# A GpSimd mask put ahead of the next pair's B, and an x load moved from GpSimd's DMA queue to SyncE's, in a fused state-space and bilinear feed-forward kernel

## The chip, the cores and the metric

The kernel runs on one core of a Trainium2 chip. Its time is device microseconds of one execution; the figure compared is the median of several executions. A profiled execution, taken apart from these, gives the trace. Times below are microseconds from the start of the profiled span unless they say otherwise.

## The reference

Inputs are `x` (4, 8, 768, 32), `a` (4, 8, 768), `B` and `C` (4, 8, 768, 16), all float32, and three weight matrices of a feed-forward part. First a state-space scan is computed for each of 4 x 8 heads, then a bilinear feed-forward layer on all heads of a token.

```python
for c in range(nc):                      # chunks of 32 tokens
    cum = np.cumsum(la, axis=-1)         # la = log(clip(a))
    L = np.exp(cum[:, :, :, None] - cum[:, :, None, :]) * causal
    CB = np.einsum('bhin,bhjn->bhij', Cc, Bc)
    y_intra = np.einsum('bhij,bhjd->bhid', CB * L, xc)
    y_inter = np.einsum('bhin,bhnd->bhid', Cc, state) * np.exp(cum)[..., None]
    y[:, :, sl] = y_intra + y_inter
    Bx = np.einsum('bhjn,bhjd->bhjnd', Bc, xc) * decay_from_j[..., None, None]
    state = decay_full[:, :, None, None] * state + np.sum(Bx, axis=2)
...
a = x @ w_a                              # x: 3072 tokens x 256, from y
b = x @ w_b                              # 256 x 1536
return (a * b @ w_out).astype(np.float32)
```

## The kernel before

The 768 tokens are cut into six blocks of 128. A block of the four batches is handled as two pairs of batches, so there are twelve pairs, p = 0 to 11; pair p belongs to block p // 2. Pairs 0 to 3 use an older layout and finish before the stretch of interest; pairs 4 and up are the ones that matter here.

For such a pair p the steps are these.

- **Loads.** `loads_bc(p)` issues the loads of C and B (128 KB each) on SyncE's queue, and `loads_x(p)` the load of x (256 KB). `loads_x` takes the issuing engine as an argument: without one it is GpSimd, with `nc.sync` it is SyncE. Both end in line 156. The natural tiles (`bn`, `cn`, `xn`) have three buffers each.
- **Scaling on GpSimd.** `scale_bc(p, 1, nc.gpsimd)` multiplies C by its decay factors into half of a `planes` tile (line 295). `scale_bc(p, 0, nc.gpsimd)` does the same for B (line 303, tile `bm`) and spreads it into the other part of `planes` with two copies (line 313). There are two `planes` tiles, for even and odd pairs.
- **Turning.** `turn(p)` is one transposing DMA on SyncE's queue (line 347) from `planes` to the tile `turned`, which holds B and C with the state dimension on partitions.
- **`prep(p)`** is scale C, scale B, turn, in that order.
- **Scores.** `scores(p)` multiplies the turned C and B on TensorE into the four banks `SC` (line 357).
- **Masks.** Each of the four banks is multiplied by the causal mask into the tile `t`. Most are done by VectorE from the bank (line 412). With `by_pool=True` ScalarE copies the bank to `tmp` (line 409) and GpSimd multiplies (line 410).
- **x.** `scale_x(p, eng)` makes x in 16 bits, on ScalarE (line 286) or GpSimd (line 288, through `prep_x`).
- **Group.** `group(blk)` computes the outputs of a block's two pairs: state times C (line 507), masked scores times x (line 418), and the sums for the next state (line 446), and lets ScalarE evacuate them to `XB` (line 537).

The feed-forward part runs between these steps on TensorE: `unit` (line 600) and `bunit` (line 666) multiply by the first two weights, VectorE forms the product, and `out_half` (line 636) and `bout` (line 693) multiply by the third. Their results go through `osb` on ScalarE (lines 648 and 705) and are stored by SyncE's queue (lines 650 and 706).

The order of everything is written out by hand: the schedule is manual, each engine and each queue runs its instructions in the order in which the program emits them, and an instruction starts when those that it depends on are done. A step's place in the program therefore also sets its place in SyncE's queue, which carries the loads, the turnings and the stores in one order. Around pair 6 that order is: loads for pairs 6 and 7, three stores of block 0 and 1, turn(6), the store of `out_store(2, 1)`, x of pair 6, turn(7), x of pair 7, C and B of pair 8, two stores, C and B of pair 9, turn(8), turn(9), x of pair 9, C and B of pair 10.

Of the kernel before, what the change touches and what calls it, by code (L numbers as in the profile page):

```python
# [28 lines left out]
def kernel(  # L29
# [13 lines left out]
    nc = tc.nc  # L43
# [92 lines left out]
    def by_token(t_):  # L136
        return t_.rearrange("p h r n -> p (h r n)").rearrange("p (t h n) -> p t h n", t=2, h=H)
# [14 lines left out]
    def load2(eng, p, which):  # L152
        if p < P0:
            return [load1(eng, p, which, bt) for bt in range(2)]
        blk, bp = divmod(p, NBP)
        return eng.dma_start(  # L156
            by_token(pair_in[p][which]).rearrange("p t h n -> p (t h) n"),
            (B, C, x)[which][2 * bp : 2 * bp + 2, :, blk * Q : (blk + 1) * Q, :].rearrange("t h q n -> q (t h) n"),
        )
# [121 lines left out]
    def scale_x(p, eng):  # L281
        X16 = mid.tile([128, H, 2, D], f16, name="x16", tag="x16")
        xo, xi = X16.rearrange("p h r d -> p (h r d)"), pair_in[p][2].rearrange("p h r d -> p (h r d)")
        st.setdefault(p, {})["X16"] = X16
        if eng is nc.scalar:
            nc.scalar.mul(xo, xi, XS)
        else:
            eng.tensor_scalar(xo, xi, XS, None, ALU.mult)  # L288

    def scale_bc(p, which, eng, factor=None):  # L290
        blk, bp = divmod(p, NBP)
        name, f = (("bm", fB), ("cm", fC))[which]
        raw = by_token(pair_in[p][which]) if p >= P0 else pair_in[p][which].rearrange("p h r n -> p r h n")
        if p >= P0 and which:
            eng.tensor_tensor(  # L295
                out=planes[p % 2][:, 4:6].rearrange("p t (h n) -> p t h n", n=N),
                in0=raw,
                in1=f[:, blk, :, bp].unsqueeze(3).broadcast_to((128, 2, H, N)),
                op=ALU.mult,
            )  # L300
            return
        m_ = mid.tile([128, 2, H, N], f16, name=name, tag=name)
        eng.tensor_tensor(  # L303
            out=m_,
            in0=raw,
            in1=(f[:, blk, :, bp] if factor is None else factor).unsqueeze(3).broadcast_to((128, 2, H, N)),
            op=ALU.mult,
        )
        st.setdefault(p, {})[name] = m_
        if p >= P0:  # L310
            dst = planes[p % 2][:, 0:4].rearrange("p (t e) (m f n) -> p t e m f n", e=2, f=2, n=N)
            for e in range(2):
                eng.tensor_copy(dst[:, :, e, :, e], m_.rearrange("p t (m f) n -> p t m f n", f=2)[:, :, :, e])
# [31 lines left out]
    def turn(p):  # L345
        T_ = mid.tile([128, 6, 128], f16, name="turned", tag="turned")
        nc.sync.dma_start(T_, planes[p % 2].rearrange("p a c -> p (a c)"), transpose=True)  # L347
        st[p]["BT"] = T_[:, 0:4].rearrange("p (t e) k -> p e t k", e=2)
        st[p]["CT"] = T_[:, 4:6]

    def scores(p):
        BT, CT = st[p]["BT"], st[p]["CT"]
        st[p]["T1"] = mid.tile([128, H, 2, Q], f16, name="t1", tag="t1")
        for e, bt, m in itertools.product(range(2), range(2), range(4)) if p >= P0 else ():
            rows = slice(32 * m, 32 * m + 32)
            c0 = (e * 2 + bt) * Q
            nc.tensor.matmul(  # L357
                SC[m][:, c0 : c0 + Q],
                BT[rows, e, bt],
                CT[rows, bt],  # L360
                start=True,
                stop=True,
                skip_group_check=True,
                tile_position=(32 * m, 0),
            )
        for e in range(2) if p < P0 else ():
            for r in range(2):
                for m in range(4):
                    for bt in range(2):
                        rows = slice(32 * m, 32 * m + 32)  # L370
                        c0 = (e * 2 + r) * Q
                        nc.tensor.matmul(  # L372
                            SC[m][64 * bt : 64 * bt + 64, c0 : c0 + Q],
                            BT[rows, e, r, bt],
                            CT[rows, bt],
                            start=True,
                            stop=True,
                            skip_group_check=True,
                            tile_position=(32 * m, 64 * bt),
                        )  # L380

    def product(p, m):

        if p >= P0:
            return (
                st[p]["T1"][:, 2 * m : 2 * m + 2].rearrange("p e t q -> p (e t) q"),
                SC[m].rearrange("p (c q) -> p c q", q=Q),
            )
        return (
            st[p]["T1"][:, 2 * m : 2 * m + 2].rearrange("p e r q -> p e (r q)"),  # L390
            SC[m].rearrange("p (e c) -> p e c", e=2),
        )
# [8 lines left out]
    def mask(out_in, by_pool=False, by_token=False):  # L401
        o_, i_ = out_in
        if by_token:
            c_ = causal_q.unsqueeze(1).broadcast_to((128, 4, Q))
        else:
            c_ = causal.rearrange("p r q -> p (r q)").unsqueeze(1).broadcast_to((128, 2, 2 * Q))
        if by_pool:
            tmp = mid.tile([128, *c_.shape[1:]], f32, name="tmp", tag="tmp")
            nc.scalar.copy(tmp, i_)  # L409
            nc.gpsimd.tensor_tensor(out=o_, in0=tmp, in1=c_, op=ALU.mult)  # L410
        else:
            nc.vector.tensor_tensor(out=o_, in0=i_, in1=c_, op=ALU.mult)  # L412
# [155 lines left out]
    def state_spread(p):  # L568
        blk, bp = divmod(p, NBP)
        if p + NBP < P0:  # L570
            Sbd = mid.tile([128, 2, H * D], f16, name="sbd", tag="sbd")
            nc.gpsimd.tensor_tensor(
                out=Sbd.rearrange("p t (m c) -> p t m c", m=4),
                in0=U32[:, p].unsqueeze(2).broadcast_to((128, 2, 4, 2 * D)),
                in1=maskbd.rearrange("p (m e) d -> p m (e d)", e=2).unsqueeze(1).broadcast_to((128, 2, 4, 2 * D)),
                op=ALU.mult,
            )
        else:
            Sbd = mid.tile([128, 2, 2 * D], f16, name="spair", tag="spair")
            nc.gpsimd.tensor_tensor(  # L580
                out=Sbd.rearrange("p t (e d) -> p t e d", e=2),
                in0=U32[:, p].rearrange("p t (e d) -> p t e d", e=2),
                in1=par.unsqueeze(1).unsqueeze(3).broadcast_to((128, 2, 2, D)),
                op=ALU.mult,
            )
        if blk + 1 < NG:
            nc.gpsimd.tensor_tensor(
                out=gU[:, p + NBP],
                in0=U32[:, p],
                in1=G[:, 2 * bp : 2 * bp + 2, blk + 1].unsqueeze(2).broadcast_to((128, 2, 2 * D)),  # L590
                op=ALU.mult,
            )
        st.setdefault(("S", p + NBP), {})["Sbd"] = Sbd
# [120 lines left out]
    def loads_x(p, eng=None):  # L714
        if p < NP:
            load2(eng or nc.gpsimd, p, 2)
# [148 lines left out]
    def prep(p, spread=()):  # L865
        if p < NP:
            scale_bc(p, 1, nc.gpsimd)
            scale_bc(p, 0, nc.gpsimd)
            turn(p)
        for q in spread:  # L870
            if q // NBP < NBLK - 1:
                state_spread(q)

    def prep_x(p):
        if p < NP:
            scale_x(p, nc.gpsimd)
# [9 lines left out]
    def stage(p, by_pool, spread=()):  # L886
        scores(p)
        if p % NBP == 0 and p // NBP + 1 < NBLK:
            fb(p // NBP + 1)
        if by_pool:  # L890
            mask(product(p, 3), by_pool=True, by_token=True)
        for q in spread:
            if q // NBP < NBLK - 1:
                state_spread(q)

    def masked(p, ms, *units):
        for i in range(max(len(ms), len(units))):
            h = units[i]() if i < len(units) else None
            if i < len(ms):
                mask(product(p, ms[i]), by_token=True)  # L900
            if h:
                h()
# [36 lines left out]
    scores(4)  # L939
    mask(product(4, 3), by_pool=True, by_token=True)  # L940
    scale_x(5, nc.scalar)
    prep(6)
    masked(4, (0, 1))
    out_mm(2, 1, o_ps, range(6, NK))
    out_store(2, 1, o_ps)()
# [1 line left out]
    go((3, 1))  # L947
    scores(5)
    mask(product(5, 3), by_pool=True, by_token=True)
    mask(product(5, 2), by_pool=True, by_token=True)  # L950
    loads_x(6, nc.sync)
    prep(7)
# [5 lines left out]
    out_half(3, 1)  # L958

    stage(6, True, (4, 5))  # L960
    loads_x(8)
    prep_x(7)
    masked(6, (0, 1))
    masked(6, (2,), *bu(2, 0, 1, 2))
# [2 lines left out]
    stage(7, True)  # L967
    loads_bc(9)
    prep(8)
    prep(9)  # L970
    loads_x(9, nc.sync)
    loads_bc(10)
# [74 lines left out]
```

## Time and profile before

| | |
|---|---|
| Median of 3 runs | 125.01 us (124.95 to 126.14) |
| Profiled execution, its own time | 125.89 us |
| Span of the profile | 124.2 us |
| TensorE busy | 117.6 us, 95% |
| VectorE busy | 85.4 us, 69% |
| ScalarE busy | 71.6 us, 58% |
| GpSimd busy | 64.2 us, 52% |
| HBM read and written | 11.13 MB and 3.15 MB |
| Loads of C and B by SyncE (128 KB), issue to landing | 4.0 and 4.3 us, medians of 8 |
| Turnings, issue to landing | 3.9 us, median of 8 |

Times of the page are from one profiled execution, which was 0.88 us longer than the median of the runs; a difference read from the trace is carried over to the median as a difference. In the profile PE is TensorE, DVE VectorE, ACT ScalarE, POOL GpSimd and SP SyncE; a `q` behind an engine's name means its sequencer or DMA queue. A row of the timeline has the start, the time, engine, line, operation, tiles and count, and in brackets the idle time of that engine just before and what ended it. For a DMA the row is the time that its issue took, not the transfer.

### The profile page before, as it was taken

The numbers are of one execution on the slowest core, as the hardware profiler recorded it, in microseconds if no ns is written. First come the engines' busy times: TensorE is split into PE (matmuls) and PEld (weight loads), VectorE is DVE, ScalarE is ACT, GpSimd is POOL, SyncE is SP. The second block draws the span as 40 slices with busy tenths as digits, with TensorE's granted clock in tenths as the row PEclk, the third lists the DMA queues.
The fourth block names the chain that finished last, engine by engine and source line by source line (L and its number), as shares of the span: only waits on it lengthen the run. The fifth ranks groups of instructions, "written<-read, shape, count | busy, mean of one in ns | idle before, by whom it ended". The sixth has DMA issues, their size and how long they took to land.

```text
span 124.2 us, 3750 instructions
## 1 busy us (share of the span) xinstructions
PE 117.6 (95%) x1471; PEld 79.9 (64%) x1471; DVE 85.4 (69%) x162; ACT 71.6 (58%) x142; POOL 64.2 (52%) x109
## 2 busy tenths in 40 slices
PE   5887999999999998999999999999999999999990
PEld 2444788988888886844457456657464775555890
DVE  1886787885978589399983989848789544747200
ACT  0464845784645684788658755683637746657220
POOL 7999699947992479467735768114920000000000
PEclk9999999999999999999999999999999999999999
DMA  3999999997989699999886797369831012010122
GB/s 66 169 154 232 171 190 132 206 154 78 98 109 224 98 97 184 110 162 134 103 136 97 54 133 135 64 68 132 176 122 48 0 42 84 5 42 0 42 84 84
DMA packets 64753, 13.73 MB, mean 111 GB/s; under 512 B 59568, under 2 KB 64336, under 8 KB 64736
## 3 DMA queue, kind: packets, MB, share of 16 engines
q1 hardware_dynamic: 60528, 9.27, 48.8%
q0 software_dynamic: 2208, 3.87, 17.8%
q10 hardware_dynamic: 2000, 0.36, 1.6%
q8 instruction: 11, 0.18, 0.6%
q14 instruction: 6, 0.05, 0.1%
HBM read 11.13 MB, written 3.15 MB: 115 GB/s over the span
## 4 chain that ended last, share of the span: by engine, by line
PE 63%; DMA 17%; POOL 7%; SPq 7%; issue 3%; DVE 1%; ACT 1%; POOLq 0%; ACTq 0%; DVEq 0%
PE ops L693 15%; PE aps L666 13%; PE bps L666 13%; DMA bn<-in_B_dram 8%; PE aps L600 6%; PE bps L600 5%; DMA Wa<-in_moe_w_a_dram 5%; PE ops L636 4%; SPq L347 4%; DMA turned<-planes 3%; SPq L156 3%; POOL bm L303 1%; PE SC L357 1%; POOL cn L147 1%; PE SC L432 1%
## 5 line engine op out<-in xcount | busy, mean ns | idle before, releaser
L614 ACT COPY asb<-aps 128x512 f32<-128x512 f32 x72 | 41.9, 586 | 15.0 <-PE aps L666 9.7
L678 DVE TENSOR_TENSOR hkb<-bps,asb 128x512 f16<-128x512 f32 x48 | 32.3, 687 | 12.9 <-ACT asb L614 11.8
L666 PE MATMUL aps<-XB,Wa 128*128 128x512 f16 x96 | 28.6, 379 | 0.0
L666 PE MATMUL bps<-XB,Wb 128*128 128x512 f16 x96 | 28.5, 379 | 0.0
L693 PE MATMUL ops<-Wo,hkb 128*128 128x256 f16 (+1 forms) x204 | 22.5, 267 | 0.0
L693 PEld LDWEIGHTS <-hkb 128*128 128x128 f16 x204 | 18.5, 98 | 3.1
L412 DVE TENSOR_TENSOR t<-SC,causal_q 128x512 f16<-128x512 f32 x26 | 16.6, 681 | 5.1 <-PE SC L357 5.1
L621 DVE TENSOR_TENSOR hk<-bps,asb 128x512 f16<-128x512 f32 x24 | 16.1, 683 | 3.5 <-ACT asb L614 3.1
L666 PEld LDWEIGHTS <-Wb 128*128 128x128 f16 x96 | 9.9, 103 | 11.0 <-issue 0.3
L666 PEld LDWEIGHTS <-Wa 128*128 128x128 f16 x96 | 9.7, 103 | 9.1 <-issue 0.2
L600 PE MATMUL aps<-X2T,Wa 128*128 128x256 f16 x96 | 14.3, 274 | 1.0 <-DMA Wa<-in_moe_w_a_dram 0.7
L705 ACT ACTIVATE osb<-ops 128x256 f32<-128x256 f32 (+1 forms) x16 | 6.0, 376 | 14.4 <-PE ops L693 14.2
L600 PE MATMUL bps<-X2T,Wb 128*128 128x256 f16 x96 | 14.1, 273 | 0.0
L288 POOL TENSOR_SCALAR x<-xn 128x512 f16<-128x512 f32 x7 | 10.4, 1489 | 6.1 <-DMA xn<-in_x_dram 5.9
L636 PE MATMUL ops<-Wo,hk 128*128 128x256 f16 x96 | 11.6, 273 | 0.0
L600 PEld LDWEIGHTS <-Wa 128*128 128x128 f16 x96 | 9.3, 104 | 2.5 <-DMA Wa<-in_moe_w_a_dram 1.2
L600 PEld LDWEIGHTS <-Wb 128*128 128x128 f16 x96 | 9.8, 103 | 0.7
L636 PEld LDWEIGHTS <-hk 128*128 128x128 f16 x96 | 8.9, 98 | 1.5 <-DVE hk L621 0.2
L412 DVE TENSOR_TENSOR t<-SC,causal 128x512 f16<-128x512 f32 x13 | 8.2, 682 | 1.8 <-PE SC L372 1.7
L303 POOL TENSOR_TENSOR bm<-bn,fB 128x256 f16<-128x256 f32 x11 | 7.0, 640 | 4.6 <-DMA bn<-in_B_dram 2.8
L410 POOL TENSOR_TENSOR t<-tmp,causal_q 128x512 f16<-128x512 f32 x6 | 6.9, 1159 | 3.7 <-ACT tmp L409 3.6
L295 POOL TENSOR_TENSOR planes<-cn,fC 128x256 f16<-128x256 f32 x8 | 5.0, 623 | 7.2 <-DMA cn<-in_C_dram 7.0
(94 smaller groups left out, 118.2 us busy)
## 6 DMA issues: line engine op xcount, KB each, us to landing
out_dram<-osb SPq DMA_DIRECT2D x23, 128.0 KB, 1.9
xn<-in_x_dram SPq DMA_DIRECT2D x6, 256.0 KB, 4.9
cn<-in_C_dram SPq DMA_DIRECT2D x8, 128.0 KB, 4.0
bn<-in_B_dram SPq DMA_DIRECT2D x8, 128.0 KB, 4.3
Wa<-in_moe_w_a_dram POOLq DMA_DIRECT2D x2, 384.0 KB, 6.9
Wb<-in_moe_w_b_dram POOLq DMA_DIRECT2D x2, 384.0 KB, 8.2
Wo<-in_moe_w_out_dram POOLq DMA_DIRECT2D x2, 384.0 KB, 6.8
xn<-in_x_dram POOLq DMA_DIRECT2D x4, 128.0 KB, 7.3
```

What stands on the lines that cost most here:

```text
L288: eng.tensor_scalar(xo, xi, XS, None, ALU.mult)
L303: eng.tensor_tensor(out=m_, in0=raw, in1=(f[:, blk, :, bp] if factor is None else factor).unsqueeze(3).broadcast_to((128, 2, H, N)), op=AL ...
L410: nc.gpsimd.tensor_tensor(out=o_, in0=tmp, in1=c_, op=ALU.mult)
L412: nc.vector.tensor_tensor(out=o_, in0=i_, in1=c_, op=ALU.mult)
L600: nc.tensor.matmul(ps[:, kk * 2 * Q : (kk + 1) * 2 * Q], W[k // 6][:, f, k % 6 // 3 * 384 : (k % 6 // 3 + 1) * 384].rearrange("p (c kk) -> ...
L614: (nc.vector.tensor_copy if on_dve else nc.scalar.copy)(asb, a_ps)
L621: nc.vector.tensor_tensor(out=s["hk"][:, 2 * k2 : 2 * k2 + 2, :].rearrange("p k q -> p (k q)"), in0=b_ps, in1=asb, op=ALU.mult)
L636: nc.tensor.matmul(o_ps[:, 0:d_model], hk[:, k, bt * Q : (bt + 1) * Q], Wo[:, k, :], start=(k == 0), stop=(k == NK - 1), skip_group_check= ...
L666: nc.tensor.matmul(t_, W[k // 6][:, f, k % 6 // 3 * 384 : (k % 6 // 3 + 1) * 384].rearrange("p (c kk) -> p kk c", kk=3)[:, k % 3], XB[:, b ...
L678: return lambda: nc.vector.tensor_tensor(out=s["hk"][:, k], in0=ps[1], in1=asb, op=ALU.mult)
L693: nc.tensor.matmul(o_ps[:, 0:w], hk[:, k, c * Q : (c + 1) * Q], Wo[:, k, cs], start=(k == 0), stop=(k == NK - 1), skip_group_check=True,)
L705: nc.scalar.activation(out=o_sb[:, 0:w], in_=o_ps[:, 0:w], func=AF.Copy, scale=1.0 / (YS * YS))
```

## The change

Two steps are moved; no arithmetic is added or removed.

First, `prep(6)`, which stood after the GpSimd mask of pair 4, is taken apart. The scaling of C of pair 6 stays there. The scaling of B of pair 6 and the turning of pair 6 now stand after the first of the two GpSimd masks of pair 5 and ahead of the second. On GpSimd the first mask of pair 5 changes places with B of pair 6. On SyncE's queue turn(6), emitted later than before, now comes behind the store of `out_store(2, 1)`.

Second, the load of x of pair 8 is no longer issued by GpSimd at the start of pair 6's stage, but by SyncE between the turnings of pairs 8 and 9.

```diff
     scores(4)
     mask(product(4, 3), by_pool=True, by_token=True)
     scale_x(5, nc.scalar)
-    prep(6)
+    scale_bc(6, 1, nc.gpsimd)
     masked(4, (0, 1))
     out_mm(2, 1, o_ps, range(6, NK))
     out_store(2, 1, o_ps)()
     masked(4, (2,), *pu(3, 0))
     go((3, 1))
     scores(5)
     mask(product(5, 3), by_pool=True, by_token=True)
+    scale_bc(6, 0, nc.gpsimd)
+    turn(6)
     mask(product(5, 2), by_pool=True, by_token=True)
     loads_x(6, nc.sync)
     prep(7)
...
     stage(6, True, (4, 5))
-    loads_x(8)
     prep_x(7)
...
     stage(7, True)
     loads_bc(9)
     prep(8)
+    loads_x(8, nc.sync)
     prep(9)
     loads_x(9, nc.sync)
     loads_bc(10)
```

## Prediction

> **What bounds the kernel now.** I read the page's busy row first, then the chain that ended last, then the waits of TensorE, then the timelines of GpSimd and of SyncE's queue around those waits.
>
> ```profile
> PE 117.6 (95%) x1471; PEld 79.9 (64%) x1471; DVE 85.4 (69%) x162; ACT 71.6 (58%) x142; POOL 64.2 (52%) x109
> ```
>
> ```profile
> PE SC L418 <- POOL t L410: 0.5, 1, 0.5
> PE SC L357 <- DMA turned<-planes: 0.2, 1, 0.2
> ```
>
> TensorE is busy for 95% of the span. The second fence is the waits of TensorE from 32 us to the end (waited for: us in total, times, longest): these two are all, and the change touches nothing before 44 us. So only two stalls can be removed: one on a mask made by GpSimd, one on a turned tile. TensorE's timeline places them:
>
> ```profile
> 48.53 0.52 PE L418 MATMUL SC<-t,x 128*32 128x128 f16 x24
> 49.52 0.29 PE L418 MATMUL SC<-t,x 128*32 128x128 f16 x8 [0.47 <-POOL t L410]
> 49.63 0.30 PE L446 MATMUL SC<-x,bm 128*32 128x64 f16 x16
> 49.87 2.79 PE L636 MATMUL ops<-Wo,hk 128*128 128x256 f16 x24
> 52.59 0.40 PE L357 MATMUL SC<-turned 32*128 32x128 f16 x16
> ...
> 68.00 0.40 PE L357 MATMUL SC<-turned 32*128 32x128 f16 x16 [0.16 <-DMA turned<-planes]
> ```
>
> The first is at 49.52, in the outputs of block 2: the last eight products wait for the second GpSimd mask of pair 5. The twenty-four before them start within 48.53 to 48.83, and at their pace the eight would start at about 48.93, so the stall is worth 0.59. The second is at 68.00, before the scores of pair 8. The last L693 matmul before it starts at 67.57; on other changes from output matmuls to scores (52.39 to 52.59) the step is 0.20, so 0.43 here hides 0.23 of waiting. From 68 to 121 TensorE is busy 53.00 of 53.00, so any shift at 68.00 goes to the end unchanged. The chain says the same: PE alone after 68.00, and DMA, SyncE's queue and GpSimd before it.
>
> **Who sets those two waits.** GpSimd:
>
> ```profile
> 43.69 1.16 POOL L410 TENSOR_TENSOR t<-tmp,causal_q 128x512 f16<-128x512 f32 x1
> 44.81 0.62 POOL L295 TENSOR_TENSOR planes<-cn,fC 128x256 f16<-128x256 f32 x1
> 46.02 0.62 POOL L303 TENSOR_TENSOR bm<-bn,fB 128x256 f16<-128x256 f32 x1 [0.59 <-DMA bn<-in_B_dram]
> 46.71 0.52 POOL L313 COPY planes<-bm 128x128 f16<-128x128 f16 x2
> 47.19 2.28 POOL L410 TENSOR_TENSOR t<-tmp,causal_q 128x512 f16<-128x512 f32 x2
> ```
>
> The reader is to see 0.59 of idling for B of pair 6 ahead of two masks whose inputs are there (ScalarE's two copies run 44.78 to 45.85). SyncE's queue:
>
> ```profile
> 46.15 2.11 SPq L650 DMA_DIRECT2D out_dram<-osb  x3
> 48.36 2.36 SPq L347 DMA_TRANSPOSE turned<-planes  x1
> 50.81 0.53 SPq L650 DMA_DIRECT2D out_dram<-osb  x1
> 51.40 0.42 SPq L156 DMA_DIRECT2D xn<-in_x_dram  x1
> 51.91 2.00 SPq L347 DMA_TRANSPOSE turned<-planes  x1
> ```
>
> The turning of pair 6 starts at 48.36, when the three stores are issued; its planes were done at 47.23. The view of the turned tile in that stretch gives 4.1 from issue to landing, so it lands at 52.45, and scores(6) start at 52.59. TensorE arrives there just in time, behind a stall of 0.59. That is the point of this case.
>
> **What the skill says.** Perfetto Trace Analysis, DMA Instruction — HWDGE: the profiled slice of an issue covers lock wait and descriptor generation; the data moves outside it. The trace agrees: 2.36 of issue, 4.1 to landing. DMA: Bandwidth & Descriptors, Queues, rings and completion order: SyncE owns one ring on each of the 16 engines, consumed in order. The trace fits (landings follow the issue order here), so what is put ahead of a turning on SyncE is ahead of it in the rings. The same page, Issuing engines are not separate DMA queues: a DMA issued elsewhere runs on the same 16 engines. So x(8) by SyncE costs the DMA engines about what it cost by GpSimd, at another time; the profile agrees in that B of pair 8 takes 6.7 to land beside x(8), against a median of 4.3.
>
> **Part 1, the order on GpSimd.** No instruction is added or removed. New order after C of pair 6: mask, B, two copies, mask. C ends at 45.43. First mask 45.43 to 46.55 (1.12 a step); B, landed by 45.9 (idle ended there), 46.55 to 47.19; copies to 47.75, with the 0.07 that stands between B and copies; second mask 47.75 to 48.91, against 49.47. The stall goes down to at most 0.05: minus 0.55. Planes of pair 6 are ready 0.52 later, at 47.75, but SyncE isn't free before 48.3: nothing. Planes of pair 7 come 0.5 earlier, behind a queue that is busy to 51.87: nothing.
>
> **Part 1, the order on SyncE.** The moved step issues a DMA too, and this is what the sum turns on. turn(6) was issued inside prep(6), ahead of out_store(2, 1); now it stands after scores(5), so that store comes first. The store's data has been there since 43.3, so it takes the place at 48.31. Its issue cost the queue 0.38 to 1.01 in the four stores of 46.15 to 51.34; I take 0.45 with the gap. turn(6) then starts at about 48.8. Its issue is stretched by what is in flight (2.36 against 1.21 where nothing is, at 68.22), so from below the delay could be nothing: the stretch shortens by what the store takes. From above it is the store's issue plus its own packets at a time when the engines are held up:
>
> ```profile
> 47.00:50.00 3.00, 2.53 (x78) 1.99 (x77) 2.46 (x5) 1.17 (x2) 3.00 (x4) 1.00 0.95 199
> 50.00:52.00 2.00, 2.00 (x20) 1.79 (x19) 1.21 (x5) 1.86 (x4) 1.15 (x4) 1.00 1.22 82
> ```
>
> The last two columns are DMA share and GB/s: from 50 to 52 the engines are fully occupied and move 82 GB/s instead of 199. So the upper bound is 0.9. I take 0.40: turned(6) at 52.85, scores(6) at 52.95 instead of 52.59: plus 0.36. The x(6) load behind both keeps its place.
>
> So the stall of 0.59 isn't gained: TensorE reaches scores(6) at 52.04 and waits 0.9 for the turning. Even with no delay of the turning the gain is only 0.09 (52.45 and 0.05).
>
> **Part 2, x(8).** GpSimd loses one issue of 1.22 at 56.33. It idles 0.68 right behind it for x of pair 7 (to 58.22), which it will do anyway: nothing on GpSimd. The DMA engines lose 256 KB between 57.5 and 62.3. B of pair 8 (issued 56.18, landed 62.9) and the store behind it (issue 4.07 at 57.68) come 1 to 2 earlier. GpSimd's B(8), at 63.06, can't go before C(8) ends at 61.53, so 0 to 1.5 earlier, copies by about 62.9, turning of pair 8 landed by about 66.6 instead of 67.95. With scores(6) 0.36 late, TensorE comes to scores(8) at 67.57 + 0.20 + 0.36 = 68.13: no wait any more. Removed: 0.23.
>
> On SyncE x(8) is issued after turn(8) (64.30 to 66.41 in before) and ahead of turn(9), which starts at 68.22 because it waits for GpSimd's copies. SyncE is idle for 1.8 between; an x load of this size costs it 0.4 to 2.0 (median 0.8). Cover: that idle time. Without it, turn(9) and all behind it are late by up to 2.0. x(8) is needed at 71.87; issued by 66.5 with the median landing of 4.9 it is there at 71.4, and x(9) had made GpSimd wait 1.1 to 74.44 anyway. C(9) and B(9), issued after the two stores, also come 1 to 2 earlier, so turn(9) is likelier earlier than later. No queue behind has less than that in hand: turned(10) lands at 81.0 for scores at 82.95.
>
> **Sum against the profiled execution** (span 124.2, time 125.89, so 1.69 around the span). Scores(6) plus 0.36, wait before scores(8) minus 0.23: plus 0.13, span 124.3. The median of the runs is 125.01, 0.88 under the profiled one; the same shift gives 125.14, rounded to 125.15.
>
> **Rivals.**
> - Forecast: turned(6) becomes the limit, 0.1 to 0.7 later. Minus 0.1 to plus 0.5: 124.9 to 125.5. For it: two queues read above. Against: the stretch of 2.36 may be a fixed date and swallow the store.
> - Gain: turning not later. Scores(6) at 52.50, minus 0.09, and minus 0.23 at 68: 124.7. At the very best, with the turning landed by 52.0, minus 0.82: 124.2. For it: planes are ready in time. Against: the store ahead.
> - Slower: x(8) stands ahead of turn(9) in the rings. In before, turned(9) lands at 72.35 (68.22 and 4.1), and TensorE needs it at 73.68, with the shift 73.8. If B(9) doesn't come earlier, the x(8) packets (256 KB; x loads in flight take about 2 between neighbouring landings) put it at 74.4: 0.6 of stall, sum plus 0.7: 125.75. It decides as soon as turned(9) lands after 73.8. For it: one queue. Against: 1.8 of idle SyncE and near-idle DMA at 67.5 to 69.
> - The change does what it says in program order; what it may not do is move the time.
>
> **Chances.** Forecast 0.65, gain 0.17, slower by turned(9) or a turning of pair 6 beyond my bound 0.18. About 1% (1.25) is what a measurement of this kernel can tell from no change; faster than that needs more than both stalls together (0.82), slower needs both mishaps at their upper ends. Range 124.5 to 126.0: the gain's nearer half below, 0.9 of late turning plus the slower rival above.
>
> **What would show it.** Right: the wait on POOL t L410 gone, a wait of 0.6 to 1.1 on the turned tile before scores(6), none at scores(8), SyncE's order store then turning at 48.3, B(8) landing under 5.5. Wrong: scores(6) at or before 52.6 (the delay term), or a wait on turned at scores(9) (the slower rival).

## The result, and the profile after

The changed kernel takes 125.69 us (median of 22 runs, 124.74 to 127.00) against 124.79 (median of 22 runs of the kernel before, 124.28 to 126.14). Medians in this document are of all runs, while each ratio with its 95% interval leaves out the slow runs, those more than 1.5% above the fastest of their kernel. The ratio is 1.0053, interval 1.0027 to 1.0079: 0.66 us slower, of which the forecast had 0.14. The profiled execution took 125.70, span 124.0, so it stands at the median, while the one of before (125.89) stands 1.1 over its median. The two spans must not be compared as they are.

The busy row of the changed kernel's page hardly moves:

```profile
PE 118.0 (95%) x1471; PEld 80.5 (65%) x1471; DVE 85.3 (69%) x162; ACT 71.6 (58%) x142; POOL 63.0 (51%) x108
```

GpSimd has one instruction less (x of pair 8). TensorE's waits from 32 us on, changed kernel (waited for: us in total, times, longest), are now a single one:

```profile
PE SC L357 <- DMA turned<-planes: 0.8, 1, 0.8
```

TensorE's timeline, changed kernel, shows where it is:

```profile
47.84 0.71 PE L418 MATMUL SC<-t,x 128*32 128x128 f16 x32
48.37 0.30 PE L446 MATMUL SC<-x,bm 128*32 128x64 f16 x16
48.60 2.79 PE L636 MATMUL ops<-Wo,hk 128*128 128x256 f16 x24
52.20 0.40 PE L357 MATMUL SC<-turned 32*128 32x128 f16 x16 [0.80 <-DMA turned<-planes]
...
67.38 0.40 PE L357 MATMUL SC<-turned 32*128 32x128 f16 x16
```

All 32 products of block 2 run in one piece, in 0.71 (0.63 where nothing is waited for): of the mask's stall less than 0.1 is left. The wait now stands at scores(6), and there is none before scores(8) at 67.38. GpSimd's timeline of the changed kernel has the new order, with no idle time that the view marks:

```profile
44.02 0.62 POOL L295 TENSOR_TENSOR planes<-cn,fC 128x256 f16<-128x256 f32 x1
44.75 1.16 POOL L410 TENSOR_TENSOR t<-tmp,causal_q 128x512 f16<-128x512 f32 x1
45.87 0.62 POOL L303 TENSOR_TENSOR bm<-bn,fB 128x256 f16<-128x256 f32 x1
46.55 0.52 POOL L313 COPY planes<-bm 128x128 f16<-128x128 f16 x2
47.04 1.16 POOL L410 TENSOR_TENSOR t<-tmp,causal_q 128x512 f16<-128x512 f32 x1
```

SyncE's queue, changed kernel, has four stores ahead of the turning instead of three:

```profile
45.34 2.46 SPq L650 DMA_DIRECT2D out_dram<-osb  x4
47.90 2.43 SPq L347 DMA_TRANSPOSE turned<-planes  x1
50.37 0.57 SPq L156 DMA_DIRECT2D xn<-in_x_dram  x1
```

The head of this execution, the stretch ahead of scores(5), ran 0.69 earlier (scores(5) at 43.57 against 44.26). Against scores(5), scores(6) come after 8.63 instead of 8.33, and scores(8) 15.18 after scores(6) instead of 15.41. That is plus 0.30 and minus 0.23, where the forecast had plus 0.36 and minus 0.23.

So TensorE's part of the sum, forecast at plus 0.13, is nearly met, at plus 0.07. That doesn't make 0.66. Most of the rest shows after TensorE's last matmul, which ends at 121.28 of 124.2 in before and at 120.66 of 124.0 in the changed kernel: a tail (from there to the end of the span) of 2.91 against 3.34. The instructions are the same, and so are the last stores: the very last lands 1.98 after the last matmul in both. Waits of SyncE's queue from 119 us to the end, kernel before:

```profile
SPq L706 <- ACT osb L705: 1.8, 2, 0.9
SPq L1042 <- DMA out_dram<-osb: 1.4, 3, 0.7
```

and the changed kernel, whose closing line is 1044:

```profile
SPq L1044 <- DMA out_dram<-osb: 1.8, 1, 1.8
SPq L706 <- ACT osb L705: 0.9, 1, 0.9
```

At the closing line SyncE checks the DMA semaphores, counters that tell that a DMA has landed, one after the other. In before it waits three times, each time for one of the last stores as it lands. In the changed kernel it waits once, for 1.8, and does its other checks after that. In the trace's records the DMAs that SyncE and ScalarE issue take eight semaphores in rotation, and the closing checks go through these in a fixed order, about 0.06 apart. Before, there are 72 such DMAs and the very last store falls on the eighth semaphore: from its landing to the closing drain, the instruction behind the checks, 0.08 pass. With x of pair 8 moved to SyncE there are 73, the last store falls on the first semaphore, and seven checks follow its landing: 0.51. The difference, 0.43, is the growth of the tail, and no term of the forecast had it.

### The profile page after: what moved, and what is told of

Read it like the earlier page. It is cut to its first block, busy times and chain, and to the rows that moved or that the text cites. A ratio compares the mean times of both kernels' runs of the same rounds, so it can differ in the third digit from the quotient of the medians.

```text
span 124.0 us, 3749 instructions
## 1 busy us (share of the span) xinstructions
PE 118.0 (95%) x1471; PEld 80.5 (65%) x1471; DVE 85.3 (69%) x162; ACT 71.6 (58%) x142; POOL 63.0 (51%) x108
## 3 DMA queue, kind: packets, MB, share of 16 engines
q1 hardware_dynamic: 62592, 9.53, 49.1%
q0 software_dynamic: 2128, 3.61, 16.7%
## 4 chain that ended last, share of the span: by engine, by line
PE 88%; DMA 3%; POOL 3%; ACT 1%; issue 1%; DVE 1%; POOLq 0%; ACTq 0%
PE ops L693 17%; PE aps L666 17%; PE bps L666 17%; PE aps L600 8%; PE bps L600 8%; PE ops L636 7%; DMA turned<-planes 3%; PE SC L219 3%; PE SC L357 2%; PE SC L418 1%; PE SC L372 1%; POOL bm L303 1%; POOL t L410 1%; PE SC L432 1%; PE fps L248 1%
## 5 line engine op out<-in xcount | busy, mean ns | idle before, releaser
L412 DVE TENSOR_TENSOR t<-SC,causal_q 128x512 f16<-128x512 f32 x26 | 16.7, 682 | 5.7 <-PE SC L357 5.7
L288 POOL TENSOR_SCALAR x<-xn 128x512 f16<-128x512 f32 x7 | 10.4, 1489 | 6.5 <-DMA xn<-in_x_dram 6.4
```

## The experiments

Three questions were open: which part costs what, whether the mask's stall and the late turning are there in every execution, and whether the tail comes from the number of DMAs. Ratios are to the kernel before, run on the same chip. The first three edits are shown against the changed kernel, the fourth against the kernel before.

**Part 1 alone** (part 2 undone).

```diff
-    loads_x(8, nc.sync)     # between prep(8) and prep(9)
+    loads_x(8)              # after stage(6, ...), by GpSimd, as before
```

> Only part 1: the first GpSimd mask of pair 5 ahead of B of pair 6, and the turning of pair 6 behind the store of out_store(2, 1); x of pair 8 stays with GpSimd. Theory T (the turning of pair 6 takes the mask's place): the wait on the mask (0.59 us) is gone, a wait of 0.7 to 1.1 on the turned tile stands before scores(6), which start 0.2 to 0.4 later against the start of scores(5) than before; the wait before scores(8) shrinks or goes because TensorE comes later; 0.1 to 0.3 us slower than before. Rival X (the cost is in moving x of pair 8): no slower than before, within 0.1 us.

Measured: 125.04, ratio 0.9997 (0.9964 to 1.0029). The trace has no mask stall, a wait of 0.73 before scores(6), scores(6) 8.56 after scores(5), and no wait at scores(8), all as theory T has it. The tail is 2.90. The time doesn't tell 0.1 to 0.3 us from nothing.

**Part 2 alone.**

```diff
-    scale_bc(6, 1, nc.gpsimd)
+    prep(6)
...
-    scale_bc(6, 0, nc.gpsimd)
-    turn(6)
```

> Only part 2: x of pair 8 loaded by SyncE between the turnings of pairs 8 and 9; GpSimd's order and the turning of pair 6 as before. Theory T: the mask's stall of 0.59 stays, scores(6) as before, B of pair 8 lands in under 5.5 us, no wait before scores(8); 0.2 us faster than before. Rival X: 0.5 us or more slower than before, with a wait on TensorE, or slower work, somewhere after 60 us.

Measured: 125.07, ratio 1.0013 (0.9986 to 1.0040). Both expectations missed. The wait before scores(8) was gone as expected, but in this execution so was the mask's stall, although up to this point the program is that of before (TensorE's timeline of this run):

```profile
48.08 0.63 PE L418 MATMUL SC<-t,x 128*32 128x128 f16 x32
51.48 0.40 PE L357 MATMUL SC<-turned 32*128 32x128 f16 x16
```

Scores(6) come 7.68 after scores(5); no profile here has a shorter distance. And the tail was 3.33, as in the changed kernel, for which the interval (up to 0.5 us) leaves room. That the time doesn't show it is left open. This turned the search to the tail.

**Both parts, the store behind the turning again.**

```diff
-    out_store(2, 1, o_ps)()
+    store21 = out_store(2, 1, o_ps)
...
     turn(6)
+    store21()
```

> The changed kernel, but the store of out_store(2, 1) is issued after the turning of pair 6, as before the change. Theory T: the turning of pair 6 starts and lands about 0.4 us earlier against scores(5) than in the changed kernel, the wait before scores(6) falls to about 0.5, scores(6) about 0.1 earlier than before the change, no wait at scores(8); 0.3 us faster than before and 0.4 faster than the changed kernel. Rival X: as slow as the changed kernel, 0.5 us over before.

Measured: 125.09, ratio 1.0002 (0.9971 to 1.0033). The turning lands 8.29 after scores(5) starts, 0.29 earlier than in the changed kernel (8.58), and there is no wait on it. But here GpSimd got x of pair 4 late, and a mask stall of 0.51 was back, with GpSimd's new order and no idle time in it. Scores(6): 8.37. In time it lies below the changed kernel, although the tail was 3.33 here too. The interval, which reaches to 1.0033 (0.41 us), still meets that of the changed kernel, so this isn't proof for theory T.

**The store ahead of the turning, nothing else.**

```diff
-    prep(6)
+    scale_bc(6, 1, nc.gpsimd)
+    scale_bc(6, 0, nc.gpsimd)
...
     out_store(2, 1, o_ps)()
+    turn(6)
```

> The kernel before with one thing changed: on SyncE's queue the store of out_store(2, 1) comes ahead of the turning of pair 6. GpSimd's order is untouched. Theory T: the mask's stall of 0.59 stays, the turning lands 0.3 to 0.5 later, a wait of 0.2 to 0.5 on it appears before scores(6); 0.1 to 0.4 us slower than before. Rival X: same as before within 0.1 us.

Measured: 125.02, ratio 0.9987 (0.9961 to 1.0012): no cost that can be seen; the upper end is 0.15 us. GpSimd found B of pair 6 landed and did not idle, and the mask's stall came to about 0.3, not 0.59 (the 32 products of block 2 take 0.95 where 0.63 is usual). The turning starts 0.49 behind the place that the store took from it, and scores(6) begin 0.13 later than TensorE could have started them. In this execution the late turning by itself cost a tenth or so.

**Changed and before, each once more**, in the runs of one chip.

> The changed kernel again, for a second profiled execution and a second set of times. Theory V (the mask's stall that part 1 removes is not in every execution of the kernel before, while the later turning of pair 6 is in every execution of the changed one): again a wait of 0.7 to 1.0 us before scores(6), scores(6) 8.5 to 8.7 after scores(5), and 0.2 to 0.5% slower than before. Rival R (the 0.5% was mostly scatter between sets of runs): the ratio is within 0.2% of 1.

Measured: 126.64, ratio 1.0060 (1.0029 to 1.0091). The 0.5% comes again in a second set of runs, so rival R is out. The head of the profiled execution was 2.5 longer than that of the first, so only distances are read from it: wait before scores(6) again (0.59 in the view, 0.66 of extra time), scores(6) 8.46 after scores(5), tail 3.35.

> The kernel before again, for a second profiled execution. Theory V: the wait on the mask before the last products of block 2 is shorter than the 0.59 us of the first profile (0 to 0.4), with scores(6) 7.7 to 8.2 after scores(5), where the first profile had 8.33. Rival R: the stall is again 0.5 to 0.7, scores(6) 8.3 after scores(5). Time within 0.2% of the runs of before in either case.

Measured: 125.69, ratio 1.0000 (0.9961 to 1.0040). Theory V's number was missed: the stall is longer, not shorter (waits of TensorE, then its timeline, this run).

```profile
PE SC L418 <- POOL t L410: 0.8, 1, 0.8
```

```profile
49.98 0.30 PE L418 MATMUL SC<-t,x 128*32 128x128 f16 x8 [0.78 <-POOL t L410]
53.05 0.35 PE L357 MATMUL SC<-turned 32*128 32x128 f16 x12
```

But what V says, that the stall isn't fixed, holds: three profiles with the order of before around pair 6 have 0.78, 0.47 and none. Of three more that follow below and change something elsewhere, two have none to speak of and one has 0.36. The two profiled executions with a stall are longer (126.13 and 125.89) than the one without (124.97, even with the longer tail), but only in part by the stall: their heads are longer by 0.5 to 0.6.

Two things set it: when GpSimd takes x of pair 4, a load for which it waits ahead of all these masks, and how long it idles after that. GpSimd's start on x of pair 4 in before, in before again and in part 2 alone:

```profile
42.12 1.49 POOL L288 TENSOR_SCALAR x<-xn 128x512 f16<-128x512 f32 x1 [3.36 <-DMA xn<-in_x_dram]
```

```profile
42.36 1.49 POOL L288 TENSOR_SCALAR x<-xn 128x512 f16<-128x512 f32 x1 [3.44 <-DMA xn<-in_x_dram]
```

```profile
41.06 1.49 POOL L288 TENSOR_SCALAR x<-xn 128x512 f16<-128x512 f32 x1 [2.74 <-DMA xn<-in_x_dram]
```

| profile | GpSimd takes x(4), before scores(5) starts | idle for B(6) ahead of the masks | stall on the mask | wait on the turning | scores(5) to scores(6) |
|---|---|---|---|---|---|
| before | 2.14 | 0.59 | 0.47 | 0 | 8.33 |
| before again | 2.05 | 0.82 | 0.78 | 0 | 8.64 |
| part 2 alone | 2.74 | 0.45 | 0 | 0 | 7.68 |
| changed | 2.23 | none | 0 | 0.80 | 8.63 |
| part 1 alone | 2.09 | none | 0 | 0.73 | 8.56 |
| both, store behind | 1.46 | none | 0.51 | 0 | 8.37 |

(The times are the starts in the timelines, GpSimd's L288 row against TensorE's scores. The stalls are as the view gives them; its 0.47 is the 0.59 of delay in the prediction. In part 2 alone the view puts the 0.45 down to VectorE, but B of pair 6 landed 0.16 before its end, as in before.) The first column less GpSimd's idle time up to the second mask of pair 5 puts all fourteen profiles in order: at 1.23 the stall is 0.78, from 1.46 to 1.59 it is 0.36 to 0.51, at 1.84 and 1.85 about 0.3, and from 2.03 on at most 0.13. The new order takes away B's idle time and no more: at 2.1 to 2.2 it leaves next to none of a stall that was 0.5 to 0.8 in the order of before, at 2.7 there is nothing to remove, at 1.5 a stall stays.

**TensorE's instruction fetch moved**, in both kernels. In the changed kernel's profile a fetch of TensorE's instructions (16 KB on one DMA engine, at 48.45 for 1.4) overlaps the turning of pair 6: 19 of its packets then take 1.2 to 1.7 each, the last until 51.27.

```diff
-    warmup(5, tcp)
+    warmup(1, tcp)
+    for i in range(64):      # 32-row matmuls into tb and tcp, results unused
+        bt, m = i % 2, i // 2 % 2
+        nc.tensor.matmul((tcp, tb)[m][64 * bt : 64 * bt + 64, 0:128], ...)
```

> The changed kernel with 64 small extra matmuls in place of four of the five warm-up matmuls behind the masks of pair 0, so that TensorE's later instructions stand 120 further on and its 16 KB instruction fetch at 48.4 comes 3 to 5 us earlier. Theory F (this fetch holds one DMA engine for 1 to 1.4 us and with it the turning of pair 6): the turning takes 2.8 to 3.2 from issue to landing instead of 4.2, the wait before scores(6) is under 0.2, scores(6) 7.7 to 8.0 after scores(5), 0.6 to 0.9 us faster than the changed kernel. Rival B (the turning waits for the loads and stores ahead of it in the rings): it still takes 4 or more, no change of time beyond the head's 0.2.

> The same 64 extra matmuls in the kernel before. Theory F: the turning of pair 6 lands 1 us earlier, but TensorE comes to scores(6) after the mask's stall anyway, so at most 0.2 us faster than before. Rival B: no change.

Measured: 128.22, ratio 1.0115 (1.0050 to 1.0181), and 127.74, ratio 1.0087 (1.0042 to 1.0131). The turned tile from issue to landing, changed kernel with the fetch moved:

```profile
DMA to landing us min/median/max: 2.8/2.8/2.8
```

It is 2.8 in both, against 4.3 and 4.1, and with the fetch moved no packet of the changed kernel's turning takes over 0.1: theory F is right on the turning. On the gain it is wrong. In the changed kernel's run SyncE issued the turning only at 50.13, 5.88 after scores(5) start instead of 4.33, so that it landed at 52.92 for all its speed, and a mask stall of 0.44 and a wait of 0.35 stood side by side. The fetch, now at 44.42, fell on the loads for pair 7; whether it delayed the queue is open, since in the other run, with the fetch at 44.93, the turning was issued 3.60 after scores(5). There a later fetch, at 65.72, met the turning of pair 8, which took 4.7, and TensorE waited for it. A fetch moved is a fetch on something else. The medians are about 2 us over the profiled executions (126.47 and 125.71), and 0.8 and 0.9 over them in the few runs that the ratios use (3 of 6 and 7 of 21). No profile shows where this time is, and it stays open.

**One DMA more in the kernel before, one less in the changed one.**

```diff
+    nc.sync.dma_start(spare, ph_t.ap())     # 5 KB, ahead of the last feed-forward part; unused
     bout(last - 1, 0)
```

> The kernel before with one more load of 5 KB on SyncE's queue, issued in the quiet stretch before the last block's feed-forward part; nothing uses it. Theory C (SyncE's closing checks take the eight DMA semaphores in a fixed order; with one DMA more the last store falls on the first of them, so seven checks run after its landing instead of none): 3.3 to 3.4 us from TensorE's last matmul to the end of the span instead of 2.9, 0.5 from the landing of the last store to the closing drain instead of 0.1, 0.4 us (0.35%) slower than before. Rival D (the longer tail belongs to x of pair 8 itself): tail 2.9, no change of time.

Measured: 125.23, ratio 1.0020 (1.0000 to 1.0040), 0.25 us where 0.4 was expected. The tail is 3.30, and 0.51 pass from the last landing to the drain. Its SyncE waits at the end are those of the changed kernel:

```profile
SPq L1044 <- DMA out_dram<-osb: 1.8, 1, 1.8
```

```diff
-    loads_x(10, nc.sync)
+    loads_x(10)
```

> The changed kernel, but x of pair 10 is loaded by GpSimd instead of SyncE, so that SyncE and ScalarE issue as many DMAs as before the change. Theory C: tail back at 2.9 us, 0.4 us faster than the changed kernel, that is 0.1 to 0.3 us over before. Rival D: tail 3.35 as in the changed kernel, 0.6 us over before.

Measured: 125.06, ratio 1.0005 (0.9978 to 1.0032). The tail is 2.90, 0.08 to the drain, and the waits are those of before, with both parts of the change still in:

```profile
SPq L1044 <- DMA out_dram<-osb: 1.4, 3, 0.7
```

Theory C holds in all fourteen profiles, those of before and after and of the twelve runs: the six with 73 DMAs have tails of 3.30 to 3.35, the eight with 72 have 2.90 to 2.91. X of pair 8 comes by SyncE in some of both groups, so its move isn't the cause. In time, the cost of the changed kernel isn't seen any more (the interval ends at 0.4 us). But it isn't seen either in part 2 alone and with the store behind the turning, which have the long tail: a single ratio here doesn't resolve 0.43, and this figure rests on the traces. The profile of this run also has no wait on the turning of pair 6, although the store is ahead of it: its issue took 1.21 instead of 2.43 and it landed 3.7 after its start, at 51.49 for scores(6) at 51.99. A mask stall of 0.3 stands ahead of it, but the turning would have been there without that stall too. So the late turning differs between executions as the stall does.

**Two mended versions.** First part 2 with x of pair 10 by GpSimd and x of pair 4 ahead of two stores; then the whole change with these two mends and the store behind the turning.

```diff
-    for f in stores:
-        f()
     loads_x(4, nc.sync)
+    for f in stores:
+        f()
...
-    loads_x(10, nc.sync)
+    loads_x(10)
```

> The kernel before, with part 2 (x of pair 8 by SyncE), x of pair 10 by GpSimd to keep the number of DMAs, and x of pair 4 issued ahead of the two stores of block 0 on SyncE's queue. GpSimd's order around pair 6 as before the change. If GpSimd's late masks come from x of pair 4 landing late: GpSimd takes x of pair 4 0.5 to 0.8 us earlier against scores(4), the mask's stall before the last products of block 2 is under 0.2, no wait at scores(8), tail 2.9; 0.2 to 0.5 us faster than before. If they come from B of pair 6 alone: stall as in the two profiles of before, no gain beyond 0.2.

> The changed kernel with three things mended: the store of out_store(2, 1) behind the turning of pair 6, x of pair 10 by GpSimd, and x of pair 4 ahead of the two stores of block 0. Theories T and C: no mask stall, wait before scores(6) 0.3 to 0.6, none at scores(8), tail 2.9; 0.6 to 0.8 us faster than the changed kernel, 0.1 to 0.4 faster than before. If only the tail counts: 0.4 faster than the changed kernel, 0.2 over before.

Measured: 125.68, ratio 1.0036 (1.0001 to 1.0071), and 124.85, ratio 0.9995 (0.9970 to 1.0021). In the first, x of pair 4 was early (taken 40.53, 3.88 before scores(5)), but GpSimd then idled 1.10 for ScalarE's copy of the bank, 0.43 for C and 0.76 for B of pair 6, and a stall of 0.4 stayed. SyncE had issued C and B earlier against scores(5) than in before (4.8 and 4.2 ahead for 2.7 and 2.1), but they took 5.0 and 5.7 to land, for 3.0 and 3.7. The two stores, now behind x of pair 4, landed 2.3 and 2.0 ahead of scores(5) instead of 4.7 and 4.0; ScalarE sat idle 2.66 for them, and scores(5) came 3.14 after scores(4) for 2.84. The expectation of a gain failed: what x of pair 4 gained, the stores and the next loads lost, and the kernel is 0.36% slower than before (0.45 us, of which this profile shows the 0.30 ahead of scores(5)). In the second, ScalarE waited 2.42 in the same way, but no wait of TensorE on another engine or a DMA is left after 32 us, scores(6) come 7.76 after scores(5), the tail is 2.90 and the span, 122.8, is the shortest of the fourteen profiles. In time it is 0.6% under the changed kernel's ratio, and no different from before.

## Why the prediction was right, and where it wasn't

- **Time.** 125.15 was forecast within 124.5 to 126.0, as no change; measured 125.69, or 125.67 with the ratio on the median that was then known. It lies in the range, at nearly five times the forecast shift. That the range held is in part luck: its upper end was meant for a later turning and for the slower rival, and the cost came from neither.
- **The turning takes the mask's place: right.** No stall on the mask, a wait on the turned tile (0.80 of the 0.6 to 1.1 named), SyncE's store then turning. Delay plus 0.30 for plus 0.36. The turned tile lands 8.58 after scores(5) for 8.20, so 0.38 later where 0.40 was taken: 0.23 by its later start and 0.15 by taking longer.
- **Minus 0.23 at scores(8): right for the profile compared**, and B of pair 8 lands in 4.9 instead of 6.7. But the kernel before has no wait there in its second profile (its step into scores(8) is the usual 0.20), so an execution like that one has nothing to gain here.
- **Minus 0.55 of mask stall: right in one execution, wrong as a constant.** The step took the profiled execution for the typical one, while the stall is anything from none to 0.78 in the view. The wait on the turning that takes its place differs too: 0.80, 0.73, 0.59 in the view and, with x of pair 10 by GpSimd, none. What the exchange costs on the mean the times don't resolve: part 1 alone lies between 0.36% faster and 0.29% slower than before.
- **The step that failed is "any shift at 68.00 goes to the end unchanged".** It holds up to TensorE's last matmul (77.02 after scores(5) in before, 77.09 in the changed kernel). The count of DMAs then adds 0.43 in the closing checks, which the sum had at nothing. The slower rival (the turning of pair 9 behind x of pair 8) was not what happened: there is no wait at scores(9), the turning of pair 9 landing at 68.27 for 73.06.
- The sum put right: plus 0.43 of tail, shown in the traces by adding it to one kernel and taking it from the other, and plus 0.07 from the two profiles for the rest; together 0.50, inside the interval of 0.34 to 0.99 us. The remaining 0.16 isn't settled, and the 0.07 is the difference of two executions whose stalls and waits vary by more than that.

## What to carry to other kernels

A stall that one profile shows is a sample: before a change is built on it, take a second profile and look at what the waiting engine was itself waiting for. Moving a step moves its DMA in its queue, and moving a DMA from GpSimd's queue to SyncE's changes the count in both. Look at the closing checks after any such change: here one DMA more cost 0.43 there, about as much as the stall of 0.47 that the change was to remove. The tail after the last matmul could be compared between profiles whose heads differ by up to 2.5: it is 2.90 to 2.91 in one group and 3.30 to 3.35 in the other.

## What the runs showed of the hardware

- The turning of pair 6 takes 3.5 to 4.4 from issue to landing in the twelve profiles with TensorE's instruction fetch beside it, and 2.8 in the two in which the fetch was moved away. In the changed kernel 19 of its packets take 1.2 to 1.7 each.
- The same 256 KB of x are 64 packets of 4 KB when GpSimd issues them and 2048 of 128 bytes from SyncE: the page's packets go from 64753 to 66737. The share of SyncE's queue rises by only 0.3 points (48.8% to 49.1%) and GpSimd's falls by 1.1 (17.8% to 16.7%).
- The very last store lands at the same distance from the last matmul (1.98), and yet the end of the kernel moves by 0.43 with the place, first or eighth, that its semaphore has in the closing checks.
